# Second mixture of experts: row numbers of a token list in one product, and a search that pauses while tokens are turned

## Chip, cores and metric

One Trainium2 chip, one of its cores. The metric is the device time of one launch in microseconds (us); a lower time is better. In the text PE is TensorE, DVE is VectorE, ACT is ScalarE, POOL is GpSimd and SP is SyncE.

## The reference, cut to what matters

A causal attention with decay (not touched here) gives 2304 tokens of 512 numbers. They pass through two mixtures of eight experts. The first sends each token to its best expert. The second, which this change is about, is greedy: over all (token, expert) scores in falling order, a token goes to an expert that still has room, and each expert takes exactly 288 tokens.

```python
logits = x @ w_gate
order = np.argsort(-logits.flatten())
for idx in order:
    tok, e = (int(idx) // E, int(idx) % E)
    if assigned[tok] >= 0 or counts[e] >= cap:
        continue
    assigned[tok] = e
    counts[e] += 1
for e in range(E):
    mask = assigned == e
    h = np.maximum(x[mask] @ w1[e], 0.0)
    out[mask] = h @ w2[e]
```

## The kernel before, in words

**Tiling.** The 2304 tokens lie as 128 partitions by 18 columns. `V` holds the scores of all tokens for all experts (128 x 18 x 8), `AQ` which expert a settled token is bound to, `rem` the room left in each expert.

**Phases.** The second mixture runs in eight phases, one expert each. To know the expert of a phase and its tokens, `search` (L1741) finds the score at which the next expert fills up. It takes the best expert of each token (L1770, L1772) and narrows the threshold in four rounds. In a round DVE compares scores with 32 candidates (L1753), PE counts with 18 products (L1784), DVE compares the counts with the room (`ok`, L1788), PE spreads the answer with a product by `ones8` (L1795), and DVE forms the next candidates (L1799, L1805, L1753). For phase 0 the rounds are run at the end of the first mixture instead (`rounds`, L1669 to L1725), while the scores `V` are read back from memory (L1658). After the rounds `search` marks the tokens above the threshold (`g` L1815, `hg` L1816), counts them by expert (`hc` L1819, product L1824), takes the expert that is full (`es` L1830), and strikes tokens and expert out of `V` (L1821, L1833) and `rem` (L1834).

**From search to gathers.** `hand` (L1838) forms the membership `m` (`mem`, L1850) and the expert's number, which SP reads so that weights can be loaded (L1861). `listing` (L1866) turns `m` into row numbers. Two products count the members (L1870, L1871), a scan and small operations give each member its place in the list (L1874 to L1880), one-hot forms of the place's high part (`ho`, 9 wide, L1881) and low part (`lbw`, L1885) are made, and the high part is multiplied by the token's number in two bf16 parts (`ht`, L1888). Eighteen products (L1893) sum the list: 32 partitions hold the token number of places 32h + partition, h = 0 to 8. But the gather wants 128 places in 128 partitions. So one reduction (L1897), four small operations (L1900), each of 32 partitions, and eight more (L1903) move the quarters into `idx`. Then POOL issues three indirect gathers (L1908), of 128, 128 and 32 rows; the last 32 rows are fetched as quarter rows, in 128 partitions.

**Turning.** `turn` and `prep` (L1913, L1920) bring the gathered tokens into the layout that the experts' products want. PE transposes half of the columns (four, L1933) and the quarter rows (one, L1944), ACT copies the high part (L1936, L1946), DVE takes the low part `xl` (L1940), and then the other half follows. Only two PSUM buffers (`tq`) are there, so the second half's transposes wait until DVE has read the first buffer.

**Order of the work.** Each engine takes its instructions in program order, and that order is fixed when the program is written. `Pace` holds estimated times of PE, DVE and POOL, and `Lanes.paced` puts a step of a side lane (g listing, p turning, s search, o output) between two steps of the experts' products (L733, L797) once its estimated due time has come. A step that the experts cannot do without is forced. The search may run two phases ahead, the turning one. At the start of phase 0 search and turning run alone (`go`). The weights of an expert come in eight pieces of 512 KB, which SP loads, ACT rounds (L699) and POOL completes (L703). Constants are made during attention: their DVE operations are spread one by one between attention's steps, their POOL operations are issued at once.

**Names and lines that the prediction touches.** L1660 to L1662 (`rows`: V is scaled), L1714 (`thr`), L1721 (`acc` in `rounds`), L1733, L1738, L1653 (three small copies), L1815 to L1834, L1845 (copy to `AQ`), L1870 to L1908, L1933 to L1950, and the due time of the turning, `pace.pool(4.0, pace.dve(1.7)) + 2.5` (L1911).

Of the kernel before, what the change touches and what calls it, by code (L numbers as in the profile page):

```python
# [7 lines left out]
F32 = mybir.dt.float32  # L8
F32R = mybir.dt.float32r
BF16 = mybir.dt.bfloat16  # L10
I32 = mybir.dt.int32
# [1594 lines left out]
class Moe2Quick(Moe2):  # L1606
# [15 lines left out]
    def __init__(self, tc, nc, ident, cp, rt, slow):  # L1622
# [9 lines left out]
        self.ihi = cp.tile([128, NH], I32, name="ihi")  # L1632
        nc.gpsimd.iota(self.ihi, pattern=[[1, NH]], base=-int(FAR) // 32, channel_multiplier=0)
# [3 lines left out]
        self.AQ = cp.tile([128, NT, E], BF16, name="AQ")  # L1637
        self.over = cp.tile([128, E], F32, name="over")
# [6 lines left out]
        self.lbw = cp.tile([128, 32 * NT + 96], BF16, name="lbw")  # L1645
        nc.gpsimd.memset(self.hbw[:, E * NT:], 0.0)
        nc.gpsimd.memset(self.lbw[:, 32 * NT:], 0.0)
# [4 lines left out]
    def start(self):  # L1652
        self.nc.vector.tensor_copy(self.rem, self.room)  # L1653

    def rows(self, m1):

        nc, V, b = self.nc, self.V, [128, self.NT, E]
        nc.sync.dma_start(out=V, in_=m1.x2[:, DM:DM + E].rearrange("(t p) e -> p t e", p=128))  # L1658
# [16 lines left out]
    def rounds(self, u, hb, cut, c, room, p, ps, nt, thr):  # L1675
# [9 lines left out]
        T, full = self.steps, c is not None  # L1685
        for r in range(self.R):
# [6 lines left out]
            if not full:  # L1693
                cmp(c[:, h:], u[:, h:], T)
            for t in range(nt):
                nc.tensor.matmul(q[:, :32], lhsT=hb[:, E * t:E * t + 128], rhs=c[:, t, :], start=(t == 0),
                                 stop=(t == nt - 1))
# [21 lines left out]
            if r:  # L1719
                a1 = p.tile([128, 1], F32, name="acc")  # L1720
                nc.vector.scalar_tensor_tensor(out=a1, in0=n, scalar=w, in1=acc, op0=ALU.mult, op1=ALU.add)  # L1721
# [4 lines left out]
    def open(self, ctx, x2, w1, w2, out):  # L1726
# [6 lines left out]
        nc.vector.tensor_copy(self.room2, self.mine)  # L1733
        i32 = lambda a: G[:, a:a + NT].bitcast(I32)
        self.pl, self.pi, self.hi, self.lo = G[:, 96:96 + NT], i32(128), i32(152), i32(176)
        self.ho = G[:, 200:200 + NT * NH].rearrange("p (t h) -> p t h", h=NH)
        self.parts2 = G[:, 376:408]
        nc.vector.tensor_copy(self.parts2, self.parts)  # L1738

    def search(self):  # L1740

        nc, p, NT, rt, pace = self.nc, self.p, self.NT, self.rt, self.f.pace
        V, rem, S, es, u, g, hg, acc, base = (self.V, self.rem, self.S, self.es, self.u, self.g, self.hg, self.acc,
                                              self.base)
# [12 lines left out]
        for ph in range(E):  # L1757
# [11 lines left out]
            if ph:  # L1769
# [45 lines left out]
            nc.vector.tensor_scalar(g, u if ph else self.u0, thr, None, op0=ALU.is_ge)  # L1815
            nc.vector.tensor_mul(hg, hb, bt(g))  # L1816
# [3 lines left out]
            due = pace.dve(0.9)  # L1820
# [12 lines left out]
            nc.vector.scalar_tensor_tensor(out=V, in0=be(es), scalar=-1e9, in1=V, op0=ALU.mult, op1=ALU.add)  # L1833
            nc.vector.scalar_tensor_tensor(out=rem, in0=es, scalar=1e9, in1=d, op0=ALU.mult, op1=ALU.subtract)  # L1834
            pace.dve(0.5)
            yield pace.t

    def hand(self, ph, es, new):  # L1838
# [5 lines left out]
        if ph == 0:  # L1844
            nc.vector.tensor_copy(AQ, new)  # L1845
        elif ph < E - 1:
            nc.vector.tensor_add(AQ, AQ, new)
# [18 lines left out]
    def listing(self, ph, m, due):  # L1866

        nc, p, NT, f, rt, pace, G = self.nc, self.p, self.NT, self.f, self.rt, self.f.pace, self.G
        yield due
        nc.tensor.matmul(G[:, 64:64 + NT], lhsT=rt.ones, rhs=m, start=True, stop=True)  # L1870
        nc.tensor.matmul(G[:, :NT], lhsT=self.ltm, rhs=m, start=True, stop=True)  # L1871
# [5 lines left out]
        nc.vector.scalar_tensor_tensor(out=self.pl, in0=G[:, :NT], scalar=-FAR, in1=sc, op0=ALU.add, op1=ALU.add)  # L1877
# [3 lines left out]
        nc.vector.tensor_tensor(self.ho, self.hi.unsqueeze(2).broadcast_to([128, NT, NH]),  # L1881
# [256 lines left out]
```

## Time and profile before

| | us |
|---|---|
| runs | 761.02, 761.04, 761.99; median 761.04 |
| the profiled execution, its own time | 760.19 |
| its span, first to last instruction | 758.4 |
| PE busy | 687.4 (91%) |
| POOL busy | 485.1 (64%) |
| ACT busy | 393.3 (52%) |
| DVE busy | 354.2 (47%) |

The span is the stretch between the first and the last instruction of the program on the core; 1.8 us lie around it. A timeline row has the start and the duration in us, then engine, line, operation, what is written and read with the shapes, the number of instructions merged, and in brackets the idle time of that engine before it and what ended it. A row of several instructions gives their whole time. A table by stretches gives for each engine its busy time and number of instructions; PEclk is the granted clock of TensorE as a share of 2.4 GHz, so 0.50 is 1.2 GHz.

### The profile page before, as it was taken

How to read it: one execution, taken by the hardware profiler on the slowest of the kernel's cores; microseconds unless marked ns; L12 is line 12 of the kernel's file. 1: busy time of each engine (PE TensorE's matmuls, PEld its weight loads, DVE VectorE, ACT ScalarE, POOL GpSimd, SP SyncE). 2: the span in 40 equal slices, each digit the busy share in tenths (PEclk: the TensorE clock that was granted, in tenths of full speed). 3: DMA queues.
4: the chain of work that ended last, by engine and by line, in shares of the span. 5: the costliest groups of instructions: out<-in, count | busy, mean ns of one | idle time of the engine just before them, and what ended most of it. 6: DMA issues, size and time to landing. Idle time of an engine off the chain costs nothing.

```text
span 758.4 us, 16054 instructions
## 1 busy us (share of the span) xinstructions
PE 687.4 (91%) x5691; PEld 570.4 (75%) x5691; DVE 354.2 (47%) x1388; ACT 393.3 (52%) x924; POOL 485.1 (64%) x504
## 2 busy tenths in 40 slices
PE   6999999999629999999999998299999999989993
PEld 3566565665329999999999998187978878888892
DVE  4766675866722222132232334756766565541020
ACT  5888778787215455455555551144535344454430
POOL 6557327271249676777776881259879778798761
PEclk9999999999959999999999999579999999999997
DMA  6498656230168272744835710347634716457201
GB/s 202 148 310 295 225 168 230 65 124 2 63 211 293 87 249 77 274 144 153 294 99 200 261 53 22 96 142 267 226 136 169 252 62 230 144 202 238 73 35 39
DMA packets 79397, 124.34 MB, mean 164 GB/s; under 512 B 10989, under 2 KB 43757, under 8 KB 79296
## 3 DMA queue, kind: packets, MB, share of 16 engines
q1 hardware_dynamic: 72944, 103.80, 41.5%
q0 software_dynamic: 6160, 18.97, 6.9%
q8 instruction: 49, 0.80, 0.4%
q14 instruction: 52, 0.43, 0.2%
q10 hardware_dynamic: 192, 0.34, 0.1%
HBM read 101.08 MB, written 22.18 MB: 163 GB/s over the span
## 4 chain that ended last, share of the span: by engine, by line
PE 52%; POOL 6%; issue 6%; DMA 4%; DVE 3%; ACT 0%; POOLq 0%; SPq 0%; DVEq 0%
PE ph L733 35%; PE ph L797 9%; POOL wl L703 5%; DMA xg<-x,idx 2%; PE ph L804 1%; PE tq L720 1%; PE tq L843 1%; PE sq L1784 1%; PE tq L1933 1%; DMA xs<-x,idx 1%; PE tq L1037 1%; POOL out_dram L1972 1%; DVE cmp L1753 1%; DMA xg<-xs 0%; POOL xg L1908 0%
## 5 line engine op out<-in xcount | busy, mean ns | idle before, releaser
L703 POOL TENSOR_TENSOR wl<-wraw,wh 128x1024 fp32r<-128x1024 f32 x128 | 305.1, 2398 | 85.4 <-ACT wh L699 82.5
L733 PE MATMUL ph<-xh,wh 128*128 128x288 f32 (+6 forms) x512 | 160.2, 313 | 0.6 <-ACT xh L1946 0.6
L733 PE MATMUL ph<-xl,wh 128*128 128x288 f32 (+6 forms) x512 | 153.5, 300 | 1.1 <-DVE xl L1940 1.1
L699 ACT CAST wh<-wraw 128x1024 fp32r<-128x1024 f32 x128 | 132.0, 1050 | 43.1 <-DMA wraw<-in_moe_w_dram 30.0
L733 PE MATMUL ph<-xh,wl 128*128 128x288 f32 (+6 forms) x512 | 153.0, 299 | 0.0
L737 DVE SCALAR_TENSOR_TENSOR hl<-ph,hh 128x256 fp32r<-128x256 f32 (+6 forms) x128 | 56.2, 443 | 102.5 <-ACT hh L761 58.8
L761 ACT ACTIVATE hh<-ph 128x256 fp32r<-128x256 f32 (+6 forms) x128 | 51.5, 402 | 96.2 <-PE ph L733 92.7
L733 PEld LDWEIGHTS ph<-xh,wh 128*128 128x128 f32 x512 | 97.5, 190 | 4.8 <-issue 3.4
L733 PEld LDWEIGHTS ph<-xl,wh 128*128 128x128 f32 x512 | 97.5, 190 | 2.1 <-DVE xl L1940 1.8
L174 ACT ACTIVATE z<-z,mx 128x128 f32<-128x128 f32 (+2 forms) x144 | 83.9, 583 | 28.4 <-DVE mx L177 27.8
L733 PEld LDWEIGHTS ph<-xh,wl 128*128 128x128 f32 x512 | 97.3, 190 | 0.2 <-POOL wl L703 0.2
L177 DVE CUSTOM_DVE_ANT_0 z<-ps,cx 128x128 f32<-128x128 f32 (+2 forms) x144 | 68.6, 518 | 51.2 <-PE ps L188 37.1
L733 PE MATMUL ph<-hh,wh 128*128 128x288 f32 (+6 forms) x256 | 79.2, 310 | 0.0
L733 PE MATMUL ph<-hh,wl 128*128 128x288 f32 (+6 forms) x256 | 76.7, 300 | 0.9 <-POOL wl L703 0.8
L733 PE MATMUL ph<-hl,wh 128*128 128x288 f32 (+6 forms) x256 | 76.8, 300 | 0.0
L151 POOL TENSOR_SCALAR_AFFINE_SELECT cx<-cb 128x256 f32<-128x256 f32 (+1 forms) x64 | 44.2, 725 | 42.5 <-DMA cb<-c8d 31.8
L797 PE MATMUL ph<-wh,hh 128*128 128x512 f32 x128 | 53.9, 421 | 0.0
L208 ACT COPY pt<-tp 128x512 f32<-128x512 f32 (+2 forms) x128 | 49.9, 438 | 6.8 <-PE tp L216 5.5
L216 PEld LDWEIGHTS tp<-ident,z 128*128 128x128 f32 x320 | 34.8, 141 | 21.2 <-ACT z L174 6.6
L797 PE MATMUL ph<-wh,hl 128*128 128x512 f32 x128 | 50.5, 394 | 0.0
L797 PE MATMUL ph<-wl,hh 128*128 128x512 f32 x128 | 50.2, 392 | 0.0
L188 PE MATMUL ps<-kd,qd 64*128 64x128 f32 (+3 forms) x256 | 49.6, 488 | 0.1
(340 smaller groups left out, 1191.3 us busy)
## 6 DMA issues: line engine op xcount, KB each, us to landing
wraw<-in_moe_w_dram SPq DMA_DIRECT2D x128, 512.0 KB, 5.5
cb<-c8d SPq DMA_DIRECT2D x15, 576.0 KB, 7.4
xs<-zrow SPq DMA_DIRECT2D x8, 803.1 KB
xg<-xs SPq DMA_DIRECT2D x6, 771.0 KB, 9.5
kd<-in_k_dram SPq DMA_DIRECT2D x16, 288.0 KB, 7.7
qd<-in_q_dram SPq DMA_DIRECT2D x16, 288.0 KB, 4.0
vt<-in_v_dram SPq DMA_DIRECT2D x4, 1024.0 KB
x<-zrow SPq DMA_DIRECT2D x1, 1080.0 KB
```

Source lines behind the costliest of these rows:

```text
L151: nc.gpsimd.affine_select(cx[:, :, CB0[i]:CB0[i] + w], cb[:, :, :w], pattern=[[0, 2], [-1, w]], compare_op=ALU.is_ge, fill=-8e9, base=128 ...
L174: nc.scalar.activation(z, z, AF.Exp, bias=mx[:, c:c + 1], scale=-1.0, accum_out=sm[:, c:c + 1])
L177: nc.vector.tensor_tensor_reduce(out=z, in0=p, in1=cx, scale=-0.125, scalar=3e38, op0=ALU.add, op1=ALU.min, accum_out=mx[:, c:c + 1])
L188: nc.tensor.matmul(p[:, j, o:o + w], lhsT=qd[h, 128 * i:128 * i + 128], rhs=kd[h, :w], start=True, stop=True, skip_group_check=True)
L208: self.nc.scalar.copy(o, i)
L216: nc.tensor.transpose(o, z[:, CB0[i] + 128 * kb:CB0[i] + 128 * kb + 128], self.ident)
L699: nc.scalar.copy(wh, t)
L703: nc.gpsimd.tensor_sub(wl[:, q], t[:, q], wh.bitcast(F32)[:, q])
L733: mm = lambda o, w, m, st, sp: nc.tensor.matmul(o, lhsT=w, rhs=m, start=st, stop=sp)
L737: nc.vector.scalar_tensor_tensor(out=hl[:, :W], in0=p[:, :W], scalar=0.0, in1=hh.bitcast(F32)[:, :W], op0=ALU.max, op1=ALU.subtract)
L761: nc.scalar.activation(hh[:, :W], p[:, :W], AF.Relu)
L797: mm = lambda o, w, m, st, sp: nc.tensor.matmul(o, lhsT=w, rhs=m, start=st, stop=sp)
```

## The change

- In phase 0 the three copies move away from the path: `rem` is copied by POOL ahead of the read of `V`; the other two go into a function `close`, which also holds the updates of `V` and `rem`. In phase 0 `close` is run between the list's products and the first use of their result; in the other phases right after `hand`. The update of `V` that stood ahead of the product L1824 is in `close` as well.
- In phase 0 the marked tokens are written into `AQ` at once, so the copy L1845 goes.
- In the list the multiplication by `m` (L1878) goes: a third product adds FAR to the members' places instead. The high one-hot form is 12 wide in place of 9, and the tile `ht` gets three columns of zeros at both ends.
- The list's product has 21 steps in place of 18, with a moving operand of 24 columns in four pieces, each one column of `ht` later: so all four quarters come out in their own partitions. A multiplication by `pick` and a reduction write the three columns of `idx` that the gathers read; the fourth follows behind the gathers.
- `prep` sets `busy` while tokens are turned. A search round's products, and both products' steps of `listing`, wait for it to end. The product with `ones8` inside a round does not.
- Estimated times change with it: 2.4 in place of 2.9 for the list, 0.5 in place of 1.7 from product to `idx`.
- In `rounds` the operation `acc` stands behind the next comparison.
- New constants: `far`, `pick`, `spl`, `ht`, and helpers.

```diff
     def rows(self, m1):
+        nc.gpsimd.tensor_copy(self.rem, self.room)
         nc.sync.dma_start(out=V, in_=m1.x2[:, DM:DM + E].rearrange("(t p) e -> p t e", p=128))
...
                 for r in range(self.R):
                     w, last = 1.0 / 32 ** r, r == self.R - 1
+                    while self.busy:
+                        yield pace.t + 0.2
                     for t in range(NT):
...
+            hg = self.hg if ph else self.AQ
             nc.vector.tensor_mul(hg, hb, bt(g))
...
-            nc.vector.scalar_tensor_tensor(out=V, in0=bt(g), scalar=-1e9, in1=V, op0=ALU.mult, op1=ALU.add)
-            pace.dve(0.3)
-            yield due
+            yield pace.dve(0.9)
             nc.tensor.matmul(S[:, :E], lhsT=rt.ones, rhs=hc, start=True, stop=True)
...
+            def close(ph=ph, d=d):
+                if ph == 0:
+                    nc.vector.tensor_copy(self.room2, self.mine)
+                    nc.vector.tensor_copy(self.parts2, self.parts)
+                nc.vector.scalar_tensor_tensor(out=V, in0=bt(g), scalar=-1e9, in1=V, op0=ALU.mult, op1=ALU.add)
+                nc.vector.scalar_tensor_tensor(out=V, in0=be(es), scalar=-1e9, in1=V, op0=ALU.mult, op1=ALU.add)
+                nc.vector.scalar_tensor_tensor(out=rem, in0=es, scalar=1e9, in1=d, op0=ALU.mult, op1=ALU.subtract)
+                pace.dve(0.8)
+            if ph:
+                close()
+            else:
+                self.behind = close
...
         yield due
+        while self.busy:
+            yield pace.t + 0.2
         nc.tensor.matmul(G[:, 64:64 + NT], lhsT=rt.ones, rhs=m, start=True, stop=True)
-        nc.tensor.matmul(G[:, :NT], lhsT=self.ltm, rhs=m, start=True, stop=True)
+        nc.tensor.matmul(G[:, :NT], lhsT=self.ltm, rhs=m, start=True, stop=False)
+        nc.tensor.matmul(G[:, :NT], lhsT=self.far, rhs=m, start=False, stop=True)
...
-        nc.vector.tensor_mul(self.pi, self.pl, m)
...
-        yield pace.dve(2.9)
-        q = G[:, 408:408 + 2 * NH]
-        for t in range(NT):
-            nc.tensor.matmul(q, lhsT=self.lbw[:, 32 * t:32 * t + 128], rhs=ht[:, t].rearrange("p h i -> p (h i)"),
-                             start=(t == 0), stop=(t == NT - 1))
+        yield pace.dve(2.4)
+        while self.busy:
+            yield pace.t + 0.2
+        for t in range(NT + 3):
+            rhs = bass.AP(tensor=flat.tensor, offset=flat.offset + 24 * t,
+                          ap=[list(flat.ap[0]), [26, 4], [8, 3], [1, 2]])
+            nc.tensor.matmul(q, lhsT=self.lbw[:, 32 * t:32 * t + 128], rhs=rhs, start=(t == 0), stop=(t == NT + 2))
         pace.pe(0.65)
+        if self.behind:
+            self.behind()
+            self.behind = None
-        nc.vector.tensor_reduce(i9, q[:32].rearrange("p (h i) -> p h i", i=2), axis=AX.X, op=ALU.add)
-        for j in range(4):
-            nc.vector.tensor_scalar_add(idx[32 * j:32 * j + 32, :2], i9[:, j:8:4], float(N))
-        for c, q in ((2, X2W // 128), (3, NK)):
-            for j in range(4):
-                nc.vector.tensor_scalar(idx[32 * j:32 * j + 32, c:c + 1], i9[:, 8:], float(q), float(q * N + j),
-                                        op0=ALU.mult, op1=ALU.add)
+        nc.vector.tensor_mul(w[:, :3], v, self.pick[:, :3])
+        nc.vector.tensor_reduce(idx[:, :3], self.spl[:, :3], axis=AX.X, op=ALU.add)
...
-        return self.turn(ph, xg, idx, pace.pool(4.0, pace.dve(1.7)) + 2.5)
+        nc.vector.tensor_mul(w[:, 3], v[:, 2], self.pick[:, 3])
+        nc.vector.tensor_reduce(idx[:, 3:], self.spl[:, 3:], axis=AX.X, op=ALU.add)
+        return self.turn(ph, xg, idx, pace.pool(4.0, pace.dve(0.5)) + 2.5)
```

## Rows read from the trace of the kernel before

**Rows 1.** Busy time by engine and granted clock in three stretches, columns in the first line

```profile
core 0: us, PE busy (x) PEld busy (x) DVE busy (x) ACT busy (x) POOL busy (x), PEclk, DMA share, GB/s
477.69:493.29 15.60, 2.79 (x70) 2.31 (x67) 11.84 (x60) 2.09 (x2) 4.44 (x4) 0.50 0.34 106
493.29:503.28 9.99, 8.21 (x54) 7.02 (x50) 5.38 (x20) 1.90 (x6) 3.30 (x2) 0.50 0.59 201
503.28:745.36 242.08, 235.70 (x2256) 203.66 (x2254) 121.54 (x512) 107.70 (x232) 190.68 (x125) 1.00 0.48 162
```

**Rows 2.** Who waited for whom, PE alone, 503.28 to 745.36: us, times, longest

```profile
PE tq L1933 <- DVE xl L1940: 4.8, 5, 2.2
PE tq L1933 <- DMA xg<-x,idx: 1.4, 4, 0.5
```

**Rows 3.** Timeline of DVE, from threshold to row numbers in phase 0

```profile
479.42 0.16 DVE L1714 SCALAR_TENSOR_TENSOR thr<-n,acc 128x1 f32<-128x1 f32 x1
...
479.73 0.23 DVE L1815 TENSOR_SCALAR sq<-u,thr 128x18 f32<-128x18 f32 x1
...
480.34 0.31 DVE L1819 TENSOR_REDUCE hc<-sq 128x8 bf16<-128x144 f32 x1
...
480.57 0.29 DVE L1821 SCALAR_TENSOR_TENSOR V<-sq,V 128x144 f32<-128x144 f32 x1
...
481.62 0.31 DVE L1845 CAST AQ<-sq 128x144 bf16<-128x144 f32 x1
...
482.30 0.30 DVE L1850 TENSOR_REDUCE mem<-ae 128x18 bf16<-128x144 bf16 x1
...
483.08 0.18 DVE L1874 TENSOR_TENSOR_SCAN psc<-onesf,gq 128x18 f32<-128x18 f32 x1
...
483.51 0.18 DVE L1878 TENSOR_TENSOR gq<-gq,mem 128x18 int32<-128x18 f32 x1
...
485.28 0.48 DVE L1888 TENSOR_TENSOR ht<-gq,row 128x324 bf16<-128x324 f32 x1
...
486.48 0.17 DVE L1897 TENSOR_REDUCE gq<-gq 32x9 f32<-32x18 f32 x1 [0.72 <-PE gq L1893]
...
486.69 0.64 DVE L1900 TENSOR_SCALAR idx<-gq 32x2 int32<-32x2 f32 x4
...
487.36 1.30 DVE L1903 TENSOR_SCALAR idx<-gq 32x1 int32<-32x1 f32 x8
```

**Rows 4.** Timeline of PE, same stretch

```profile
480.92 0.19 PE L1824 MATMUL sq<-hc,ones 128*128 128x8 bf16 x1 [1.77 <-DVE V L1821]
...
485.81 0.63 PE L1893 MATMUL gq<-ht,lbw 128*128 128x18 bf16 x18 [2.95 <-DVE ht L1888]
```

**Rows 5.** Groups by line on PE, 503.28 to 745.36: count | busy us, mean ns | idle before

```profile
L1784 PE MATMUL sq<-cmp,hbw 128*128 128x32 bf16 x378 | 12.9, 177 | 0.0
L1893 PE MATMUL gq<-ht,lbw 128*128 128x18 bf16 x126 | 4.3, 171 | 0.0
```

**Rows 6.** Timeline of POOL, first gather of phase 0

```profile
488.22 1.05 POOL L1908 DMA_INDIRECT xg<-x,idx  x1 [12.89 <-issue]
```

**Rows 7.** Timeline of DVE, end of the first mixture

```profile
477.72 0.35 DVE L1660 TENSOR_SCALAR V<-V,ends,unit 128x144 f32<-128x144 f32 x1 [0.29 <-DMA V<-x]
```

**Rows 8.** Timeline of PE, second half of three turnings

```profile
581.78 0.63 PE L1933 MATMUL tq<-ident,xg 128*128 128x128 f32 x4 [0.19 <-DVE xl L1940]
...
638.53 0.63 PE L1933 MATMUL tq<-ident,xg 128*128 128x128 f32 x4 [0.70 <-DVE xl L1940]
...
671.48 0.63 PE L1933 MATMUL tq<-ident,xg 128*128 128x128 f32 x4 [2.19 <-DVE xl L1940]
```

**Rows 9.** Timeline of DVE, last list

```profile
669.31 1.30 DVE L1903 TENSOR_SCALAR idx<-gq 32x1 int32<-32x1 f32 x8
```

**Rows 10.** Who waited for whom, POOL alone, the same stretch

```profile
POOL xg L1908 <- DVE idx L1900: 9.2, 3, 3.4
```

**Rows 11.** The page's costliest groups: busy, mean ns | idle before, releaser

```profile
L703 POOL TENSOR_TENSOR wl<-wraw,wh 128x1024 fp32r<-128x1024 f32 x128 | 305.1, 2398 | 85.4 <-ACT wh L699 82.5
```

More of the change, by code (lines that the diff above doesn't have):

```diff
@@ L1637, in __init__ @@
         self.AQ = cp.tile([128, NT, E], BF16, name="AQ")
+        self.far = cp.tile([128, 128], BF16, name="far")
+        nc.vector.tensor_scalar_mul(self.far, ident, FAR)
+        j4 = iota_f(nc, cp, "j4", [[0, 1]], 0, 1)
+        jq = cp.tile([128, 1], F32, name="jq")
+        nc.vector.memset(jq, 0.0)
+        for k in (32, 64, 96):
+            g1 = cp.tile([128, 1], F32, name=f"jq{k}")
+            nc.vector.tensor_scalar(g1, j4, float(k), None, op0=ALU.is_ge)
+            nc.vector.tensor_add(jq, jq, g1)
+        self.pick = cp.tile([128, 4, 4, 2], F32, name="pick")
+        self.spl = cp.tile([128, 4, 9], F32, name="spl")
+        jj = iota_f(nc, cp, "jj4", [[1, 4], [0, 2]], 0, 0)
+        for c, a in enumerate((1.0, 1.0, float(X2W // 128), float(NK))):
+            nc.vector.tensor_scalar(self.pick[:, c], jj, jq, a, op0=ALU.is_equal, op1=ALU.mult)
+            if c < 2:
+                nc.vector.memset(self.spl[:, c, 8:], float(N))
+            else:
+                nc.vector.tensor_scalar_add(self.spl[:, c, 8:], jq, a * N)
+        self.ht = cp.tile([128, NT + 6, 12, 2], BF16, name="ht")
+        nc.gpsimd.memset(self.ht[:, :3], 0.0)
+        nc.gpsimd.memset(self.ht[:, NT + 3:], 0.0)
         self.over = cp.tile([128, E], F32, name="over")
@@ L1652, in start @@
     def start(self):
-        self.nc.vector.tensor_copy(self.rem, self.room)
+        pass
     def rows(self, m1):
         nc, V, b = self.nc, self.V, [128, self.NT, E]
+        nc.gpsimd.tensor_copy(self.rem, self.room)
         nc.sync.dma_start(out=V, in_=m1.x2[:, DM:DM + E].rearrange("(t p) e -> p t e", p=128))
@@ L1683, in cmp @@
                                     op=ALU.is_ge)
-        T, full = self.steps, c is not None
+        T, full, keep = self.steps, c is not None, None
         for r in range(self.R):
@@ L1694, in rounds @@
                 cmp(c[:, h:], u[:, h:], T)
+            if keep:
+                keep()
+                keep = None
             for t in range(nt):
@@ L1720, in rounds @@
                 a1 = p.tile([128, 1], F32, name="acc")
-                nc.vector.scalar_tensor_tensor(out=a1, in0=n, scalar=w, in1=acc, op0=ALU.mult, op1=ALU.add)
+                keep = lambda a1=a1, n=n, w=w, acc=acc: nc.vector.scalar_tensor_tensor(
+                    out=a1, in0=n, scalar=w, in1=acc, op0=ALU.mult, op1=ALU.add)
                 acc = a1
@@ L1832, in search @@
             self.hand(ph, es, hg)
-            nc.vector.scalar_tensor_tensor(out=V, in0=be(es), scalar=-1e9, in1=V, op0=ALU.mult, op1=ALU.add)
-            nc.vector.scalar_tensor_tensor(out=rem, in0=es, scalar=1e9, in1=d, op0=ALU.mult, op1=ALU.subtract)
-            pace.dve(0.5)
+            def close(ph=ph, d=d):
[8 more added lines that the diff above has]
+                close()
+            else:
+                self.behind = close
             yield pace.t
@@ L1843, in hand @@
         ae = p.tile([128, NT, E], BF16, name="ae")
-        if ph == 0:
-            nc.vector.tensor_copy(AQ, new)
-        elif ph < E - 1:
+        if 0 < ph < E - 1:
             nc.vector.tensor_add(AQ, AQ, new)
@@ L1910, in listing @@
                 bounds_check=a.shape[0] - 1, oob_is_err=False)
-        return self.turn(ph, xg, idx, pace.pool(4.0, pace.dve(1.7)) + 2.5)
+        nc.vector.tensor_mul(w[:, 3], v[:, 2], self.pick[:, 3])
+        with nc.allow_low_precision(reason="row numbers below 2 ** 24"):
+            nc.vector.tensor_reduce(idx[:, 3:], self.spl[:, 3:], axis=AX.X, op=ALU.add)
+        return self.turn(ph, xg, idx, pace.pool(4.0, pace.dve(0.5)) + 2.5)
     def turn(self, ph, xg, idx, due):
@@ L1927, in prep @@
         f.px, f.pk = (xh, xl), 0
+        self.busy = True
         def half(k0):
@@ L1958, in prep @@
         f.pk = NK
+        self.busy = False
         return xh, xl
```

42 lines of the change are left out of this document (22 added, 20 removed).

## The prediction, made before the changed kernel was run

> **What bounds the kernel now.** I read first the table of busy time by stretches [rows 1], because the change touches two stretches with different limits. From 477.69, where the scores have been read back, to 493.29, where the first tokens are turned, PE works 2.79 of 15.60 us: nothing but the chain from scores to gathers runs, on DVE, and each 0.1 us cut from it starts phase 0 0.1 us earlier. From 493.29 to 503.28 PE works at a granted clock of 0.50 (1.2 GHz), from 503.28 on at 1.00. From there to 745.36 PE works 235.70 of 242.08 us: PE is the bound, and only its 6.4 us of idle time and its own instructions count. The list of waits says where these lie [rows 2]: all in the transposes of the turning (L1933), 4.8 us behind `xl` on DVE, in five of seven turnings, and 1.4 us behind the landing of gathers. Last I followed the chain in the timelines [rows 3 to 6].
>
> **The chain before phase 0.** (1) Without the three copies `g` starts about 0.04 after `thr` ends (the step from L1897 to L1900 has that gap), so at 479.62, not 479.73 [rows 3]: -0.11. The copy given to POOL runs while POOL waits 12.89 us for the row numbers [rows 6]; its other two copies come back in `close`. (2) The product L1824 waits for the update of `V`, over at 480.86, though its operand `hc` is done at 480.65 [rows 3, 4]: -0.21. SP reads the expert's number earlier by what is saved up to there, so two pieces of weights are asked for earlier; nobody waits for that. (3) Copy to `AQ`: 0.31 and a gap of 0.03: -0.34. (4) The scan stands behind the updates of `V` and `rem`; `mem` is done at 482.60, two products and their latency (0.06 and 0.19 as at L1824, 0.04 for reading) and one product more end at about 482.93, not 483.08: -0.15. (5) Multiplication by `m`: 0.18 and 0.04: -0.22. (6) Wider forms: from 144 to 324 elements an operation grows from 0.30 to 0.48 [rows 3], 1.0 ns an element; 54 and 108 more cost +0.16. (7) Three more products: 4.3 us / 126 = 34 ns each with 18 columns, 12.9 / 378 = 34 ns with 32 [rows 5], so 24 columns cost the same: +0.10. The new operand is read in pairs, with gaps, which no row shows: at nothing extra the bound is 0.10, at twice the price of each of 21 products it is 0.82; I take 0.10, as width did not matter either. (8) Row numbers: from 486.48 to the end of L1900 at 487.33 are 0.85 us; a multiplication and a reduction of some 25 elements, each as the reduction of 0.17 with its 0.04, take 0.38: -0.47. Eight more operations of 1.30 us lay behind and go too, which starts the search for phase 1 earlier; that search is not what phase 0 waits for. (9) `close`, two updates of 0.29 and three small operations, about 0.85, lies beside the products (DVE waited 0.72 there, and 0.10 is added): 0; without that cover +0.85. Sum: -1.24. The first gather starts 0.90 after its row numbers [rows 3, 6], which I leave as it is.
>
> At (2) `hc` now reads SBUF instead of PSUM. The rows have 0.31 for the reduction of 144 elements out of PSUM and 0.30 for one out of SBUF [rows 3], so nothing is taken for it. [...]
>
> **What it is worth.** The 1.24 us are kept whole if the return of the clock moves with the products, and halved if it stays at 503.28, since what is done meanwhile runs at half speed: 0.62 to 1.24. I take -1.0.
>
> In `rounds` the moved `acc` saves nothing: its chain ends behind the scaling of `V`, for which DVE waits 0.29 on the read [rows 7]. The constants are made during attention, where POOL has room and DVE operations are spread one at a time; I take 0 (up to +0.3).
>
> **The PE-bound stretch.** Added: in seven lists three products and the one with FAR, 4 x 34 ns x 7 = +0.95. Removed: waits for `xl`. What waits is the second half's transposes, for the first buffer; what stands in front on DVE is the search's or the list's work. In three turnings it followed products that `prep` now holds back: 0.19, 0.70, 2.19 [rows 8]; the last had the twelve operations on row numbers in front, 1.30 of them in L1903 [rows 9]. No engine waits for `busy`: it only moves these products behind the turning in PE's order, and the search, which has until the next phase, takes the delay. These 3.1 us go; behind the search's held product stand only later search steps. The other 4.8 - 3.1 = 1.7 us came from an answer (product by `ones8`, then the comparison) to a round begun before the turning. That product is not held back, so I leave them. The bounds are -2.2 (only the longest goes, the others return elsewhere as the steps shift) and -4.8; I take -3.1, what the rows give turning by turning. Next in line there is the landing of the gathers. The planned due time of a turning moves 1.7 - 0.5 = 1.2 us ahead, the real row numbers only 0.47, so transposes stand 0.73 us nearer to the landing where gathers wait for the numbers and not for POOL's other work: three lists [rows 10]. From 0 to 3 x 0.73 = 2.2; one had slack, so I take +1.0. POOL's splits queued behind those gathers have the 3 us to spare that POOL idles there.
>
> **Sum.** -1.0 - 3.1 + 0.95 + 1.0 = -2.15. The profiled execution took 760.19 (span 758.4 and 1.8 around it), so 758.0; the median of the runs is 0.85 higher, so 758.9. Differences under 0.2% (1.5 us) cannot be told from none here.
>
> **Rivals.** *All waits go and the clock returns early* (0.15). With searches held back PE's stream is denser at the start of phase 0. The clock came back only at 503.28, after a stretch in which PE worked 8.21 of 9.99 us [rows 1]; if it came back 2.5 us sooner, 1.25 us more are won. With 4.8 for `xl` and no new wait for gathers: -1.24 - 1.25 - 4.8 + 0.95 = -6.3, 754.7. Against it: PE still waits for the same ACT and DVE steps there. [...]
>
> *The search is late for phase 1* (0.17). The turning of phase 0 now holds the search, so list 1 comes later between the experts' products; if it slips behind one more split of 2.4 us on POOL [rows 11], gathers and turning of phase 1 slip too, and PE has nothing else: -2.15 + 2.4 = +0.25, 761.3, no change.
>
> *The pause does not pause what matters* (0.13). If in each turning the unguarded answer stands before `xl`, the 4.8 stay: -1.0 + 0.95 + 1.0 = +0.95, 762.0, no change.
>
> *The turning is asked for too soon* (0.10), the rival on the other side. PE takes transposes in order, so a gather that has not landed stops the experts too. If all seven turnings meet it by 0.73, the wait grows by 5.1 and not 1.0: -1.0 - 3.1 + 0.95 + 5.1 = +1.95, 763.0. It decides for slower from a growth of 4.7 on. For it: four waits are there already [rows 2]; against it: in the early phases gathers wait for POOL, whose estimate is unchanged.
>
> **How the numbers follow.** The forecast has 0.45. Its own range, by the bounds above, is 756.5 to 760.5, so some 0.07 of it lie within 0.2%. Faster: 0.38 + 0.15 and a little of the two middle rivals, 0.58. The same: 0.28. Slower: 0.14, the last rival and upper ends. The range of 754.5 to 762.5 leaves out the last rival and the far end of the first.
>
> **What would show it.** Right: first gather of phase 0 at 487.0; eight L1903 operations gone and `idx` ready 0.4 after the products; waits for `xl` near 1.7, for gathers near 2.4; lists of 21 products at 34 ns. Wrong: products of the list over 50 ns; PE idle at the start of phase 1; waits for `xl` still near 4.8; idle time between 503 and 745 that has grown; a chain before the first gather no shorter.

## The result, and the profile after

The changed kernel takes 768.28 us (median of six runs, 765.33 to 769.61) against 761.03 of the kernel before: a ratio of 1.0086, 95% interval 1.0067 to 1.0105. It is slower by some 7 us, where 758.9 was forecast and 762.5 was the upper end of the range. The profiled execution took 767.97 with a span of 766.2, that is 7.8 more than before.

The span divides into four parts. The scaling of `V` starts at 480.51, not 477.72 [rows 7]: 2.79 are lost before the stretch that the change was about. From there to the start of the first expert product of phase 0 (498.59, before 495.27) it is 18.08 in place of 17.55: +0.53. From there to the start of the last product of the phases it is 254.54 in place of 250.09: +4.45. What follows is the same.

Busy time by stretches after, with the columns of [rows 1] and its three stretches first, then one short stretch inside the last:

```profile
480.48:496.20 15.72, 3.02 (x73) 2.46 (x69) 10.93 (x50) 2.09 (x2) 4.42 (x4) 0.50 0.35 106
496.20:506.44 10.24, 8.20 (x45) 6.36 (x46) 3.30 (x11) 1.90 (x6) 3.32 (x2) 0.50 0.55 182
506.44:753.13 246.69, 239.33 (x2285) 205.06 (x2285) 114.55 (x449) 107.97 (x232) 190.60 (x125) 0.99 0.48 160
588.36:591.78 3.42, 3.42 (x9) 2.56 (x9) 0.00 (x0) 0.53 (x1) 2.95 (x2) 0.50 0.52 125
```

In the long stretch PE is idle for 7.36 us, not 6.38, and it works 3.6 us more. The last line tells 1.7 of these: for 3.42 us the granted clock is 0.50, and the products of L797 in it start 0.43 us apart, where 0.23 is usual outside it. (No view gives the clock in GHz; 512 columns in 0.427 us are 1.2 columns per ns, with which the 1.2 GHz in the text ahead agrees.) Before, it had not fallen between 503.28 and 745.36.

PE's waits in the long stretch (`xr` are the quarter rows), to be held against [rows 2]:

```profile
PE tq L1977 <- DMA xg<-x,idx: 3.2, 5, 0.9
PE tq L1988 <- DMA xr<-x,idx: 2.7, 2, 1.6
PE tq L1977 <- DVE xl L1984: 1.3, 1, 1.3
```

The waits for `xl` fell from 4.8 to 1.3, as forecast. The waits for gathers rose from 1.4 to 5.9.

**The chain before phase 0.** Timeline of DVE, from the scaling of `V` and the threshold to the row numbers:

```profile
480.51 0.35 DVE L1684 TENSOR_SCALAR V<-V,ends,unit 128x144 f32<-128x144 f32 x1 [0.27 <-DMA V<-x]
...
482.21 0.16 DVE L1741 SCALAR_TENSOR_TENSOR thr<-n,acc 128x1 f32<-128x1 f32 x1
...
483.09 0.41 DVE L1848 TENSOR_REDUCE hc<-AQ 128x8 bf16<-128x144 bf16 x1
484.24 0.17 DVE L1854 CUSTOM_DVE_ANT_0 d<-sq,rem 128x8 f32<-128x8 f32 x1 [0.74 <-PE sq L1850]
...
488.24 0.16 DVE L1862 COPY sq<-mine 128x8 f32<-128x8 f32 x1
489.13 0.20 DVE L1863 COPY gq<-parts 128x32 f32<-128x32 f32 x1 [0.73 <-PE gq L1934]
...
489.79 0.16 DVE L1866 SCALAR_TENSOR_TENSOR rem<-sq,d 128x8 f32<-128x8 f32 x1
489.87 0.17 DVE L1942 TENSOR_TENSOR spl<-gq,pick 128x24 f32<-128x24 f32 x1
490.07 0.18 DVE L1944 TENSOR_REDUCE idx<-spl 128x3 int32<-128x27 f32 x1
```

The two products of PE on which DVE waits there, and the subtraction (`d`) as it stood before:

```profile
483.56 0.19 PE L1850 MATMUL sq<-hc,ones 128*128 128x8 bf16 x1 [1.61 <-DVE hc L1848]
...
488.38 0.72 PE L1934 MATMUL gq<-ht,lbw 128*128 128x24 bf16 x21 [2.73 <-DVE ht L1924]
```

```profile
481.15 0.17 DVE L1828 CUSTOM_DVE_ANT_0 d<-sq,rem 128x8 f32<-128x8 f32 x1 [0.28 <-PE sq L1824]
```

From the end of `thr` to the end of the row numbers it is 7.88, not shorter than the 7.75 of [rows 3]. Two rows took the gain. `close` does not run beside the list's products: its second copy writes into the PSUM tile that they write, and waits 0.73 for them, so that 0.74 of `close` (489.13 to 489.87) come behind the products. And the subtraction starts 0.50 after the product that it waits for (over at 483.74); before it started at 481.15, 0.04 after the end of the product of [rows 4].

**Attention.** PE had no wait over 0.06 us between 36 and 60 us before. After, it has two, and DVE makes the new constants at that time. First PE's timeline, then DVE's:

```profile
45.46 0.33 PE L288 MATMUL tp<-ident,ot 128*128 128x128 f32 x1 [1.27 <-ACT pt L208]
...
48.48 0.33 PE L246 MATMUL tp<-ident,z 128*128 128x128 f32 x1 [1.27 <-DVE x L289]
```

```profile
42.41 0.56 DVE L311 TENSOR_TENSOR jq<-jq,jq 128x1 f32<-128x1 f32 x1
...
43.35 0.46 DVE L311 TENSOR_SCALAR pick<-jj,jq 128x8 f32<-128x8 f32 x2
43.64 0.55 DVE L177 CUSTOM_DVE_ANT_0 z<-ps,cx 128x384 f32<-128x384 f32 x1
...
46.61 0.69 DVE L311 TENSOR_SCALAR pick<-jj,jq 128x8 f32<-128x8 f32 x1
...
47.28 0.81 DVE L311 TENSOR_SCALAR room<-de 128x8 f32<-128x8 f32 x1
```

L311 is where held-back constants are issued, one per step. They are 52 operations in place of 34: the last one starts at 47.28, before at 37.11, and one on eight elements takes up to 0.81 us there. That they are what PE waits for is tried below (e1).

**A turning with its gathers late.** PE, then POOL, in the turning of phase 3's tokens:

```profile
584.67 0.33 PE L1977 MATMUL tq<-ident,xg 128*128 128x128 f32 x1
585.69 0.55 PE L1977 MATMUL tq<-ident,xg 128*128 128x128 f32 x3 [0.70 <-DMA xg<-x,idx]
587.32 0.33 PE L1988 MATMUL tq<-ident,xr 128*128 128x128 f32 x1 [1.07 <-DMA xr<-x,idx]
...
588.18 0.48 PE L797 MATMUL ph<-wh,hh 128*128 128x512 f32 x1
588.46 0.63 PE L797 MATMUL ph<-wl,hh 128*128 128x512 f32 x1
```

```profile
577.99 2.40 POOL L703 TENSOR_TENSOR wl<-wraw,wh 128x1024 fp32r<-128x1024 f32 x1
580.55 1.05 POOL L1948 DMA_INDIRECT xg<-x,idx  x1 [0.16 <-issue]
...
583.23 1.00 POOL L1948 DMA_INDIRECT xr<-x,idx  x1 [0.30 <-issue]
```

A split stands in front of the gathers, the transposes follow the first gather by 4.1 us, PE waits twice, and then its products take longer: the fall of the clock. (After the waits of lists 4, 5 and 6, of 1.5, 1.0 and 1.6 us, it does not fall; what makes it fall is not shown.) Gathers are also under way longer than before; the listing of DMA issues gives medians of 4.6 and 4.2 us from issue to landing, before 4.2 and 3.0:

```profile
xg<-x,idx POOLq DMA_INDIRECT x16, 4.6
...
xr<-x,idx POOLq DMA_INDIRECT x8, 4.2
```

In two lists the longer landing goes with more traffic. Busy time in the stretches of their gathers; the last two numbers are DMA's share and GB/s:

```profile
636.00:646.00 10.00, 9.01 (x96) 8.39 (x95) 4.66 (x19) 4.71 (x12) 8.80 (x9) 1.00 1.06 363
683.00:689.00 6.00, 6.00 (x38) 5.47 (x37) 1.60 (x6) 4.56 (x10) 5.00 (x4) 1.00 0.34 98
```

In the first the gathers landed 6.4 to 7.8 us after their start, in the second after 3.5. Before, the one list in such traffic (627.00 to 635.20, 363 GB/s) took 6.3 to 6.6.

### The profile page after: what moved, and what is told of

Read it like the earlier page. It is cut to its first block, busy times and chain, and to the rows that moved or that the text cites. A ratio compares the mean times of both kernels' runs of the same rounds, so it can differ in the third digit from the quotient of the medians.

```text
span 766.2 us, 16044 instructions
## 1 busy us (share of the span) xinstructions
PE 691.8 (90%) x5723; PEld 571.6 (75%) x5723; DVE 351.0 (46%) x1324; ACT 393.3 (51%) x924; POOL 485.8 (63%) x511
## 4 chain that ended last, share of the span: by engine, by line
PE 51%; issue 7%; DMA 6%; POOL 4%; DVE 1%; ACT 0%; POOLq 0%; SPq 0%
PE ph L733 33%; PE ph L797 10%; POOL wl L703 3%; DMA xg<-x,idx 3%; PE ph L804 2%; DMA xr<-x,idx 1%; PE tq L843 1%; PE tq L720 1%; PE tq L1977 1%; DMA wraw<-in_moe_w_dram 1%; PE sq L1812 1%; DMA xs<-x,idx 1%; PE tq L1037 1%; POOL xg L1948 1%; PE gq L1934 0%
## 5 line engine op out<-in xcount | busy, mean ns | idle before, releaser
L797 PE MATMUL ph<-wh,hh 128*128 128x512 f32 x128 | 55.0, 430 | 0.0
L797 PE MATMUL ph<-wh,hl 128*128 128x512 f32 x128 | 51.1, 399 | 0.0
L797 PE MATMUL ph<-wl,hh 128*128 128x512 f32 x128 | 51.0, 398 | 0.0
```

Source lines behind the costliest of these rows:

```text
L797: mm = lambda o, w, m, st, sp: nc.tensor.matmul(o, lhsT=w, rhs=m, start=st, stop=sp)
```

## The experiments

They ran in seven jobs, each beside the kernel before. In one job that kernel takes 762.6, near the 761.0 of the comparison above (**first kind**); in six it takes 772 to 775 (**second kind**). What sets the kind is not known; the same chip number stood once for each. Ratios are to the kernel before of the same job; "phases" is the time from the start of the first to the start of the last expert product of the second mixture, "idle" is PE's idle time there. Both come from one profiled execution of each run. A part of their scatter is the clock: it comes back 5.5 us (g3) to 11.0 us (e1) after the first product, in the first comparison 7.9, before 8.0.

| run | kind | ratio [95%] | phases | idle |
|---|---|---|---|---|
| change, first comparison | 1 | 1.0086 [1.0067, 1.0105] | 254.5 | 8.6 |
| b1, kernel before | 1 | 1.0004 [0.9989, 1.0019] | 250.0 | 7.4 |
| g1, three mends | 1 | 1.0046 [1.0028, 1.0064] | 254.9 | 10.0 |
| g2, turning earlier | 1 | 1.0171 [1.0136, 1.0206] | 259.4 | 11.6 |
| g3, lists not held | 1 | 1.0055 [1.0035, 1.0075] | 252.9 | 8.1 |
| c1, change again | 2 | 0.9990 [0.9970, 1.0009] | 256.6 | 11.1 |
| e1, constants later | 2 | 0.9998 [0.9983, 1.0014] | 257.4 | 10.4 |
| e2, close beside | 2 | 0.9974 [0.9960, 0.9989] | 258.9 | 10.6 |
| f1, three mends, other places | 2 | 0.9963 [0.9943, 0.9984] | 257.2 | 11.3 |
| e3, due 1.7 | 2 | 1.0068 [1.0044, 1.0092] | 265.9 | 16.1 |
| f2, f1 and due 1.7 | 2 | 1.0069 [1.0048, 1.0089] | 268.0 | 16.5 |
| d1, g1 and due 1.7 | 2 | 1.0027 [1.0010, 1.0045] | 260.0 | 12.8 |
| d2, g1 and due 2.9 | 2 | 0.9911 [0.9888, 0.9934] | 252.0 | 7.0 |
| d3, the same | 2 | 0.9898 [0.9870, 0.9926] | 252.1 | 7.0 |
| d4, the same | 2 | 0.9914 [0.9884, 0.9943] | 249.7 | 7.1 |
| l1, change and due 2.9 | 2 | 0.9918 [0.9897, 0.9939] | 253.7 | 7.5 |
| e4, no pause | 2 | 1.0035 [1.0022, 1.0047] | 259.9 | 15.6 |
| h1, no pause, due 1.7, mends | 2 | 0.9993 [0.9979, 1.0008] | 257.5 | 12.5 |
| p1, before and pause | 2 | 1.0011 [0.9988, 1.0035] | 260.8 | 14.1 |

**Controls.** The unedited change (c1) and the unedited kernel before (b1).

> The changed kernel, nothing edited, beside the kernel before on the chip of this job (the first four experiments ran on a chip where the kernel before takes 772.5 and not 761.0). Theory (the loss belongs to the program): a ratio between 1.006 and 1.011. Rival (it depends on the chip, on how fast transfers and answers come): a ratio between 0.998 and 1.004.

> The kernel before, unedited, for its profile on the chips of the experiments (where it takes 772 to 774 and the changed one 773.4, ratio 0.999). Theory (attention's loss is the same everywhere, and there the phases repay it because waits for the search's answers are longer): attention 2.2 to 2.6 shorter than with the change (its last scores at 182.0 to 182.2), the stretch from the first to the last product of the phases 260 to 261, that is 3 to 4 longer than the 257.0 of the changed kernel. Rival (the phases are as long, and what is gained lies in the stretch before them): phases within 1 of 257.0, and 3 us more between the read of the scores and phase 0.

The rival of c1 holds: in a job of the second kind the same program is no slower than the kernel before. b1 met the first kind, so that its numbers do not answer; it repeats the profile of before, waits of 4.8 and 1.4 included. What differs between the kinds shows in one search round. In c1, PE's products, POOL's issues and DVE's answer:

```profile
588.61 0.62 PE L1812 MATMUL sq<-cmp,hbw 128*128 128x32 bf16 x18
588.87 1.02 POOL L1948 DMA_INDIRECT xg<-x,idx  x1 [0.31 <-issue]
...
590.20 1.00 POOL L1948 DMA_INDIRECT xr<-x,idx  x1 [0.30 <-issue]
591.15 0.25 DVE L1816 TENSOR_SCALAR ok<-sq,room 128x32 bf16<-128x32 f32 x1 [2.21 <-PE ph L733]
...
591.68 0.18 PE L1823 MATMUL sq<-ok,ones 128*128 128x32 bf16 x1 [1.57 <-DVE ok L1816]
```

DVE starts 1.9 us after the products' end at 589.23, and PE then waits for DVE. The same round of the same program in the first comparison, with a gather issued at the same moment:

```profile
581.66 0.62 PE L1812 MATMUL sq<-cmp,hbw 128*128 128x32 bf16 x18
...
581.90 1.02 POOL L1948 DMA_INDIRECT xg<-x,idx  x1 [0.31 <-issue]
...
582.31 0.25 DVE L1816 TENSOR_SCALAR ok<-sq,room 128x32 bf16<-128x32 f32 x1 [0.33 <-PE sq L1812]
```

There it starts 0.03 after. In the phases of c1 an engine that waits for PE gets the signal 0.6 to 3.3 us after the product's modelled end in 13 places, 12 of which overlap a gather or scatter that POOL issues; the changed kernel of the first comparison, the same program, has no such place. In e1 and f1, two other jobs of the second kind, 12 such instructions each are late by more than 0.5, all beside such an issue, and in g1, whose phases are the same program, none of them is.

**Constants.** Edit of e1, which holds the new operations back to later items of attention's loop (f1 has "c" in place of "g", which gives two per item and not five; g1 is as here):

```diff
-            if i > 0:
+            if i in (1, 2) or i > 5 and k == "g" or i == 3 and len(slow.calls) > 18:
                 slow.issue(1)
```

> The changed kernel with the 18 new DVE operations of the constants held back: they are issued five per item of attention from its seventh item on, in place of one per step between 40 and 48 us. Theory (they cost the 2.8 us that attention lost): both waits of 1.27 us between 45 and 49 us go, the scaling of V starts 2.5 to 2.9 us earlier (near 477.8), and the kernel takes 765.5, 2.8 less than the changed one. Rival (the spread of landings of the masks from DRAM made the two waits, not the constants): the waits stay or move, the scaling of V stays within 0.5 of 480.5, and the time stays at 768.3.

Both waits of 1.27 are gone; between 36 and 60 us PE waits for nobody. Attention's last scores come at 182.44, in c1 at 184.40, before at 182.18; `V` is scaled at 480.71 against 483.27 in c1. (The 477.8 expected was a number of the first kind; between attention and the first mixture e1 takes 45.3, the first comparison 43.2.) A new wait at 98 us keeps 0.65. So in the first pair of profiles attention and what follows lost 2.6 to 2.8, and between c1 and e1 2.0 to 2.6 come back. Over all profiles, of both kinds, the last scores come at 184.1 to 184.8 in the six with the constants as made, at 182.4 to 183.6 in eight of nine with e1's places (186.9 in d1), at 182.2 to 183.0 in the three of the kernel before, p1 included. By the middle values the constants cost 1.8, and 1.6 come back; the rest of the 2.6 is scatter between executions. The time does not show them: 0.9998 beside 0.9990 in another job, phases 0.8 longer.

**The chain.** Edit of e2:

```diff
-        nc.gpsimd.tensor_copy(self.rem, self.room)
+        nc.vector.tensor_copy(self.rem, self.room)
...
-        self.parts2 = G[:, 464:496]
+        self.parts2 = S[:, 352:384]
```

> The changed kernel with the second copy of the steps put into the PSUM tile of the search, not into that of the list, and the copy of the room made by DVE while it waits for the scores, not by POOL. Theory (the chain before phase 0 lost 0.73 to close behind the list's products and 0.45 to the second semaphore of the subtraction): from the end of thr to the end of idx 6.85 instead of 8.04, the subtraction starts 0.25 after the product in place of 0.74, close ends before the last product of the list, and phase 0 starts 1.1 earlier; the kernel takes 767.2. Rival (DVE and not the two waits sets the pace there, since close takes 0.85 wherever it stands, or the semaphore of POOL is not what the subtraction waited for): the step stays above 7.5, and the time within 0.5 of 768.3.

Timeline of DVE in e2:

```profile
486.70 0.17 DVE L1854 CUSTOM_DVE_ANT_0 d<-sq,rem 128x8 f32<-128x8 f32 x1 [0.28 <-PE sq L1850]
...
490.88 0.20 DVE L1863 COPY sq<-parts 128x32 f32<-128x32 f32 x1
...
491.68 0.15 DVE L1866 SCALAR_TENSOR_TENSOR rem<-sq,d 128x8 f32<-128x8 f32 x1
...
491.96 0.18 DVE L1944 TENSOR_REDUCE idx<-spl 128x3 int32<-128x27 f32 x1
```

The theory holds for the chain: the subtraction starts 0.04 after its product, the copy waits for nothing, and from `thr` to the row numbers it is 6.85. `close` ends 0.28 after the last product, at 491.55, so the cover is a little short. The subtraction starts 0.50 after its product in all six profiles with the copy on POOL, and 0.04 after it in all eleven of the changed kernel with the copy on DVE. That a second semaphore makes the difference is a reading; only the place of the copy was varied. The ratio is 0.0016 (1.2 us) below that of c1, of another job.

**The mends together**, constants, chain and `rem`.

> The changed kernel with three mends: the 18 constants spread over later items of attention (two per item), the second copy of the steps in the search's PSUM tile, the room copied by DVE. Theory (attention's 2.8 and 1.1 of the chain come back whole): 3.5 to 4 us under the unedited change of the same job, a ratio 0.0046 to 0.0053 lower. Rival (an earlier start of the phases is lost again to gathers and to the clock's return): no more than 2.3 us under it.

> The three mends with the constants placed as in the run that held them back to the seventh item (five per item), not two per item. Theory (the places decide: two per item gave attention nothing back, its last scores at 184.41 as without a mend, five per item gave 182.44): last scores at 182.3 to 182.6, phase 0 at 498.5 or earlier, and 1.8 to 2.2 us under the three mends with two per item, a ratio of 0.9935. Rival (what attention wins is lost later, since the clock's return and the transfers set the phases): a ratio of 0.996 as before.

f1 is 0.0027 below c1, no more than the rival gave: with two constants per item the last scores come at 184.41, as without a mend. g1 met the first kind, where it stands at 1.0046 beside the 1.0086 of the unedited change: 3 us come back, about what e1 and e2 had shown for the two parts (1.6 to 2.6, and 1.0); its last scores come at 183.01, in b1 at 182.71. The ratio of 0.9935 that its theory gave was for the second kind, and was not tried there. What is left is in the phases: 254.9 against 250.0 in b1 of the same job. PE's waits in g1:

```profile
PE tq L1977 <- DMA xg<-x,idx: 5.8, 9, 1.2
PE tq L1988 <- DMA xr<-x,idx: 2.8, 3, 1.1
PE tq L1977 <- DVE xl L1984: 1.3, 1, 1.3
```

**When the turning is asked for.** One number is edited: `pace.dve(0.5)) + 2.5` becomes `pace.dve(0.5)) + 1.3` (g2), `pace.dve(1.7)) + 2.5` (e3, f2, d1) or `pace.dve(2.9)) + 2.5` (d2, d3, d4, l1).

> The changed kernel with the old due time of the turning (1.7 in place of 0.5 behind the list's products). Theory (the turning is asked for too soon, by the 1.2 us of the planned time): PE's waits for gathers in the turnings of phases 1 to 6 fall from 5.9 to between 1 and 2.5, the clock does not fall near 588, and the kernel takes 763 to 765. Rival (the pause makes the lists late, so that their gathers stand behind one more split on POOL; the due time is not it): the waits for gathers stay above 4 and the time above 767.

> The three mends and the old due time of the turning (1.7 in place of 0.5). Theory, from the run of the old due time alone (1.0068 where the changes of attention and chain gave 0.9974 to 0.9998): a later turning holds the search back longer, PE then waits for the search's answers, and the kernel takes 5 to 8 us more than the three mends alone. Rival (waits for gathers are what is left, and that run was an accident of its chip): 2 to 4 us less than the three mends alone, waits for gathers below 2.5.

> The three mends, with the turning asked for 1.2 us earlier still (1.3 in place of 2.5 behind the gathers). Theory (a turning that holds the search is better early: 1.2 later cost 8 us): 1 to 3 us less than the three mends alone. Rival (the gathers are not there: waits for gathers grow by up to 1.2 in each of six turnings): 2 to 6 us more, waits for gathers above 4.

PE's waits in g2:

```profile
PE tq L1977 <- DMA xg<-x,idx: 8.8, 12, 2.5
PE tq L1988 <- DMA xr<-x,idx: 2.1, 1, 2.1
```

In the first kind 1.2 us earlier raises the waits for gathers from 8.6 to 10.9; the clock falls for 6.8 us at 648.7 and for 3.4 at 679.4, and the ratio goes from 1.0046 to 1.0171. The rival holds, by more than it gave: an earlier turning costs there. In the second kind the opposite edit, 1.2 us later, also costs, 0.8% in e3 against c1 (two jobs) and 1.1% in f2 against f1. Waits for gathers are small there (0.5 in e3), but PE waits up to 3.4 us at a time for the search, whose answers come late, and the clock falls three times inside the phases of each, for some 10 us in all in e3 and 17 in f2, half of which is lost (in c1 it does not fall, in f1 for 3.4). So neither the theory nor the rival of e3 held whole: its waits for gathers fell, further than the theory said, and its time rose.

> The three mends (places as in the last job) and the old due time of the turning. Theory (on a chip like that of the record, where PE's answers come at once, the phases lose to gathers asked for too soon; 1.2 us earlier still cost 10): waits for gathers fall from 7.4 to between 1.5 and 3.5, phases 250.5 to 252.5 long, and 3 to 4.5 us less than the three mends alone, a ratio between 0.999 and 1.001. Rival (the search, held by a later turning, is late, as on the two slower chips, where this due time cost 8): phases 258 or longer, ratio above 1.006. On a chip with before near 773 the rival's number is expected again.

> The three mends and a due time 1.2 us later than the old one (2.9). Theory (gathers): waits for gathers below 0.8, another 1 to 2 us less than with the old due time, a ratio of 0.996 to 0.999. Rival (what is held by the pause comes too late from here on): the search of some phase ends after its turning should begin, PE waits at the end of a phase for the next one's tokens, and the time is 2 or more above the old due time's.

> The three mends with the due time of 2.9 once more, unedited, for a chip like that of the record. Theory (waits for gathers are what the phases of the changed kernel lose there, and a turning 2.4 us later meets them all): where the kernel before takes 761 to 763, waits for gathers below 1, phases 249 to 251 long, a ratio of 0.992 to 0.996; that beats both kernels. Rival (the later due time only moved the search away from POOL's issues on the slow chip): a ratio of 0.999 or above there. Where the kernel before takes 772 to 774, the ratio of 0.991 again.

> The three mends with the due time of 2.9, unedited, in a third job, since the last two met slow chips. Theory (gathers asked for too soon are what the phases lose on a chip like that of the record): where the kernel before takes 761 to 763, waits for gathers below 1, phases 249 to 251 long, a ratio of 0.992 to 0.996. Rival: a ratio of 0.999 or above there. Where the kernel before takes 772 to 774, between 0.988 and 0.992 again.

> The changed kernel with the due time of 2.9 and no other edit: the loss of attention and of the chain stays in. Theory (gathers asked for too soon are the phases' loss on a chip like that of the record; elsewhere the later turning takes the search's rounds away from POOL's issues): where the kernel before takes 761 to 763, no wait for gathers above 0.5 in all, phases 249 to 251 long, a ratio of 1.001 to 1.004, that is 3.5 to 5.5 us less than the change as made; where it takes 772 to 774, a ratio of 0.994 to 0.997, the three mends being worth some 3 us. Rival (the mends, not the due time, made the last three runs fast): 1.007 or above on the one kind of chip, 0.999 or above on the other.

All five met the second kind. At 1.7 (d1) the kernel is 0.3% above the one before, less than the rival's 0.6, with phases of 260 as the rival said; at 2.9 it is 0.9 to 1.0% below it, three times. l1 shows that in the second kind the due time gives this, not the mends: without them it is 0.8% below. Two of its waits, and what is left for gathers, phase 0 included:

```profile
PE sq L1823 <- DVE sq L1819: 3.2, 2, 2.6
PE tq L1977 <- DVE xl L1984: 1.8, 3, 0.8
PE tq L1977 <- DMA xg<-x,idx: 1.4, 3, 0.7
```

In c1 the answers cost PE 6.4 (3.4 and 3.0), here 3.2. Due times of 0.5, 1.7 and 2.9 give 0.9990, 1.0068 and 0.9918 on the unedited rest, in three jobs: no trend. That each gives another order of instructions, which meets POOL's issues or misses them, is a reading that no run tries by itself. No later due time met the first kind.

**The pause.** Left out in e4 and h1 (with the due time of 1.7), alone in p1; g3 leaves out the two loops of `listing`.

```diff
-        while self.busy:
-            yield pace.t + 0.2
```

> The changed kernel without the pause (the three loops on busy left out). Theory (the pause does what it says, and the early due time makes the waits for gathers): waits for xl rise from 1.4 to between 4 and 5, waits for gathers stay within 1.5 of 5.9, and the kernel takes 769 to 772. Rival (the pause makes the lists late, and so the gathers): waits for gathers fall below 3, waits for xl rise by no more than 3, and the kernel takes 766 to 768.

> The three mends with the old due time and without the pause: the shorter listing alone. Theory (of the change only the listing and the early start are left; the pause was worth 3.1 us of waits for xl): waits for xl 4 to 5 as before, waits for gathers 1.5 to 2.5, a ratio of 0.998 to 1.001, and 1 to 3 us above the same kernel with the pause. Rival (the pause gives nothing on such a chip, because what it holds makes lists and gathers late): at or below the kernel with the pause.

> The kernel before with the pause alone (the flag in the turning and the three loops). Theory (the pause removes the waits for xl that followed products of search and list, 3.1 us, and costs nothing): waits for xl near 1.7, a ratio of 0.996. Rival (held search and lists come later, the gathers with them): waits for xl fall, waits for gathers or for the search's answers grow by as much or more, a ratio of 1.000 or above.

> The three mends with the search held during a turning, but not the lists (two of the three loops left out). Theory (the list is what the gathers wait for, so holding it costs): gathers of the lists that met a turning start up to 3 us earlier, and the kernel takes 1 to 3 us less than the three mends alone. Rival (no list meets a turning, since the list of a phase comes after its turning is over): the same program order and the same time within 0.5.

Against its counterpart the pause is worth 0.45% (e4 against c1, two jobs), costs 0.34% (h1 against d1, one job) and changes nothing that can be told (p1). Waits for `xl` are larger without it each time: 6.7 in e4 and 5.9 in h1 with those of phase 0, against 2.7 in c1 and 3.9 in d1; 5.9 in b1 against 2.2 in p1, of the other kind. That half of the theory holds; what the held work does elsewhere is as large (in p1 PE waits 4.9 for the search's answers and 2.3 for a list). Not holding the lists gives the same time as holding them, 1.0055 beside 1.0046, with phases 2 us shorter in the profiled execution.

## Why the prediction was wrong

**The chain: mechanism half right.** Steps (3) to (7) came out within 0.05 each, and so did (8), which takes 0.38 once `close` is over. Steps (1) and (2) gave 0.16 together, not 0.32: without the copies `g` still starts 0.11 after `thr` and not 0.04, and the reduction to `hc` took 0.41 out of SBUF (`AQ`, bf16) and not 0.31 as out of PSUM (`sq`, f32), so 0.10 more where nothing was taken. Both read across the inner order of their tile; whether the place or the type makes the difference was not tried. Step (9) failed: "lies beside the products". The bound without cover, 0.85, was nearly the true one (0.74 behind the products), for a reason that stood in the diff: the copy and the products share one PSUM tile (the copy waits 0.73 there, and for nothing in e2, where it writes into another tile). A wait of 0.46 at the subtraction was in no step. The copy given to POOL was costed at nothing because POOL is free, and it is done 8 us early (POOL's row ends at 476.14); but with it the subtraction starts 0.46 later (by the reading above, for a second semaphore). e2 removes both waits and reaches 6.85, 0.90 under the kernel before. Of the -1.24 forecast, +0.14 was measured. The clock's return moved with the first product (3.16 and 3.32 later), so a gain there would have been kept nearly whole; it came 7.9 after that product, before 8.0, so the early return of the first rival is not there. Its 2.5 us were an assumption, and no run shows that a denser stream brings the clock back sooner; nor was the stream denser: in the stretch that ends with its return PE worked 8.20 of 10.24 us, in the kernel before 8.21 of 9.99.

**Constants in attention: the step that failed by size.** "I take 0 (up to +0.3)" was argued from the room on POOL and from the spreading, one operation per step. What DVE does at the place where the queue of 34 ends, and who waits for it there, was in no step. In the first comparison 2.8 were lost ahead of the chain; e1 shows the place, and all profiles together a cost of some 1.8.

**Waits for `xl`: right in sum and in kind, partly by luck turning by turning.** 3.1 forecast, 3.5 measured, and p1, the pause alone, has 1.1 of the 4.8 left in the turnings. The one that is left, 1.31 in the turning of list 5, stands behind an answer, as the step had it. But it was to be left, with 0.45, in lists 2 and 4, where both are gone.

**Waits for gathers: outside its bounds.** "+1.0, from 0 to 2.2" became +4.5. The step counted three lists in which gathers wait for the row numbers. But the lists with late landings are 3 to 6, where gathers stand behind a split or travel beside weights. The rival "the turning is asked for too soon", with 5.1 at most, is a part of it, and g2 shows its sign. Counted from the end of the list's products, the transposes start 0.86, 0.84 and 0.65 sooner than before in lists 3, 5 and 6, and 0.28 later in list 4. So, by an estimate from these, at most 2.4 of the 4.5 are the due time's. The rest are later landings: in list 4 the gathers start 2.61 behind the end of the products, before 1.23, behind a split and a scatter; in list 6 the third gather is under way 7.3, before 4.5. No run parts the two in the first kind. What no step had either: in list 3 the clock fell after the waits, 1.7 us more.

**Added products: right in size.** 147 products take 4.9 us, 33 ns each, where 34 were taken.

Together: +2.8 attention, +0.1 chain, +0.4 in the landing of phase 0's gathers, and in the phases +4.5 waits for gathers, -3.5 for `xl`, +1.7 clock, +0.8 products (0.6 and seven with FAR), which leaves 1.0 of their 4.5. That lies in the products of the second layer (L797): outside the fall, 63 of them in place of 50 take some 0.31 to 0.34 us to the start of the next where the usual one takes 0.23, nearly all of them (61 of the 63, all of the 50) beside a product of another kind.

**What stays open.** Why there are two kinds of jobs. Whether the due time of 2.9, or of 1.7, pays in the first kind; there only an earlier one was tried. So how much of the phases' loss is the due time's is in part argued. The version with the three mends and 2.9 beats both kernels in three jobs of the second kind (766 to 767 against 774).

## What to carry to other kernels

Constants "made while there is time" are placed like any other work: look at what the engine does at the end of the queue that they lengthen, and whether the next engine waits there (here PE did, twice 1.27 us). Before work is moved beside another engine's, compare the tiles: here a copy into one part of a PSUM tile waited 0.73 us until PE had written another part. And where transfers set a wait, an estimate that moves only the consumer forward can buy a wait (1.2 us earlier in g2 took the waits for gathers from 8.6 to 10.9 us): read the landings, not the issue times.

## What was not expected of the hardware

A copy on POOL that was done 8 us before still cost 0.46 at the instruction of DVE that reads its result and waits for PE, in six profiles of six. In c1, e1 and f1, of the second kind, PE's signals reached the waiting engines up to 3.3 us late, in 36 of 37 places while POOL issued an indirect transfer; in the changed kernel of the first comparison no place in the phases was as late as 0.5 us. It is an observation, its cause was not tried.
